# Modulation columns in two halves of the features, two of the k projections in two groups of matmuls, and a new order of the whole program

## The chip, the cores and the metric

The kernel runs on one core of a Trainium2 chip. The metric is the device time in microseconds (us) of one execution; three executions of the kernel before took 556.19 to 556.42 us, median 556.39. PE is TensorE, with PEld its loads of weights; DVE is VectorE, ACT is ScalarE, POOL is GpSimd, SP is SyncE, which here only issues DMAs.

## What is computed

An adaptive layer norm block on x of 2048 x 512: modulation vectors from a condition `c`, then linear attention with a learned softmax feature map of 32 heads, then a spatial-shift mixer with an MLP. Cut to its core:

```python
mod = (_silu(c) @ w_mod).reshape(1, 6, 1, 512)
sa, ca, ga, sb, cb, gb = (mod[:, i] for i in range(6))
h = _layernorm(x) * (1 + ca) + sa
q, k, v = h @ wqkv                           # per head: 16 columns each
pq, pk = q @ w_phi, k @ w_phi                # per head, 16 x 16
phi_q = concat([softmax(pq), softmax(-pq)])  # phi_k from pk in the same way
o = phi_q (phi_k^T v) / (phi_q phi_k^T 1)
x = x + ga * (o @ wo)
h = _layernorm(x) * (1 + cb) + sb
g = shift(gelu(_layernorm(h) @ w1)) @ w2     # quarters of the features shifted by +1, -1, +2, -2 rows
x1 = h + g
x = x + gb * (x1 + gelu(_layernorm(x1) @ w3) @ w4)
```

## The kernel before, in words

**Numbers.** Large products run in a fast float32 format. Each operand is split into a high part, a rounded copy, and a low part, the rest (`hi_lo`, L483: a copy and a subtraction), and each product is three matmuls (`three`, L474). Small products and transposes take plain float32; each of those matmuls shows in the trace as two records.

**An order that is written out.** The program is first recorded as a list of operations (`Plan`, `plan.op`, L314), each with its engine, what it reads and what it writes. Then it is emitted in the order of the printed table `ORDER` (L40), in which each number is an operation's index in that list and a letter behind it puts the operation on another of the engines that may do it (A for ACT, V for DVE, G for POOL). A second table, `SLOT`, names the buffer that each tile gets. Each engine works off its own operations in this order. So the order on each engine, the order of the DMAs on SP and the reuse of buffers are all set by the two tables; nothing is decided at run time but the waits. Tiles that share a kind of buffer (`KIND`, L34) can wait for each other: the kind `s2` holds raw weights, modulation rows, inputs and normed inputs alike, and `ps` is the eight PSUM banks (`pp`, `pt`, `pa`, `ac`).

**DMAs.** Loads go through `load` (L447) to SP's queue. Eight semaphores are used in turn, so a DMA is issued only after the eighth one before it has landed, besides waiting for its buffer.

**The start, up to the first projection.**
- `warm` (L500): nine groups of four matmuls on a tile of ones. Their results aren't used. What follows on TensorE stands behind them in the order.
- `load_folded` (L648), for wk and then wq: the feature map's 16 x 16 matrices are multiplied into the weights. For each of four blocks of 128 rows: a load of 256 KB (`rk`), four matmuls of 128 x 128 with a block-diagonal tile (`bd`) into a bank `pp`, and `hi_lo` into the weight tiles `w`.
- `layernorm` of the first four tiles of x (`xl` to `xn`).
- `mod_cols` (L529): the columns sa and 1 + ca that scale the first norm. silu(c) is spread to 32 columns (`wide`). Four loads of 512 KB bring 128 rows each of the first 1024 columns of w_mod (`mod2`); for each, four matmuls of 32 x 256 run beside each other in four strips of 32 rows of one bank. The bank is copied to SBUF (`r`), two transposes turn it into columns, and two `ts` write `cols`.
- `h_chunk` (L685) for chunk 0: transposes of `xn` into `pt` (two banks in turn, each for two of the four blocks of features), scale by 1 + ca and bias by sa, `hi_lo` into `hh`.

**The rest.** `proj` (L712) is 12 matmuls of 128 x 512 (four blocks of features, three each). Per chunk of two tiles `k_feat`, `v_feat` and `q_feat` project and take their softmaxes, and `kv_add` accumulates phi_k^T v in PSUM. Beside them run the rows of modulation (`mod_acc`, `mod_rows`), further loads and preparations of weights. Then come the attention's output, `pp<-w,oT` (wo), the second norm, `pa<-nT,w` (w1), `pp<-w,sh` (w2), and the MLP: `pa<-bH,wq` (w3) and `ac<-w,gg` (w4).

Of the kernel before, what the change touches and what calls it, by code (L numbers as in the profile page):

```python
# [11 lines left out]
OP = mybir.AluOpType  # L12
# [3 lines left out]
P = 128  # L16
NK = D // P
# [5 lines left out]
TPC = CH // P  # L23
# [141 lines left out]
)  # L165
SLOT = {
    "pp": "354206170301136260517505607442523070157475601660106031401453313745662015634523405103645651314210"
          "4326265450622670302462",
    "bd": "c3",
    "w": "124657de12834c6d075e18",  # L170
    "rk": "9768efjh",
# [1216 lines left out]
```

## Time and profile before

| | value |
|---|---|
| device time, median of 3 (lowest, highest) | 556.39 us (556.19, 556.42) |
| profiled execution: device time, span | 556.38 us, 554.6 us |
| instructions | 12399 |
| bytes moved, mean rate | 124.90 MB, 225 GB/s |
| granted TensorE clock, mean | 0.999 |

The span runs from the first to the last instruction of the engines; about 1.8 us of the device time lie around it. In the rows of the profile a name such as `pp<-w,hh` reads "into `pp` from `w` and `hh`", and `128*128 128x512` is a matmul of a 128 x 128 weight tile on 512 columns. Matmuls are pipelined, so that the mean duration of one is longer than the distance between two.

### The profile page before, as it was taken

What the parts mean: (1) busy time and instruction counts of PE and PEld (TensorE: products, weight loads), DVE (VectorE), ACT (ScalarE), POOL (GpSimd) and SP (SyncE); (2) the same over time, 40 slices, a digit from 0 to 9 for tenths busy, and PEclk for the clock granted to TensorE, in tenths of its full rate; (3) what the DMA queues carried; (4) which work ended last, traced back from release to release, by engine and by line L of the source; (5) the groups of instructions that cost most, each with busy time, mean ns of one, the idle gap of its engine ahead of it and who ended that gap; (6) DMA issues with size and microseconds to landing.
All of it is one profiled execution on the core that took longest, in us unless ns stands there. A gap on an engine that the chain in (4) does not pass through costs nothing.

```text
span 554.6 us, 12399 instructions
## 1 busy us (share of the span) xinstructions
PE 548.3 (99%) x4522; PEld 491.5 (89%) x4522; DVE 484.6 (87%) x901; ACT 352.1 (63%) x833; POOL 339.5 (61%) x348
## 2 busy tenths in 40 slices
PE   9999999999999999999999999999999999999997
PEld 8888788888777788888889999999999999999996
DVE  3899997999999999999898788788788777888876
ACT  4789988644344788978888786867352535235540
POOL 3289849788799999986986533516334453133522
PEclk9999999999999999999999999999999999999999
DMA  8964651654765668687898888896976796572212
GB/s 317 386 215 148 212 161 42 214 173 143 247 193 158 221 212 232 238 294 256 269 298 267 274 297 276 281 324 250 382 232 241 264 379 204 174 249 93 59 58 76
DMA packets 63749, 124.90 MB, mean 225 GB/s; under 512 B 7140, under 2 KB 26852, under 8 KB 59592
## 3 DMA queue, kind: packets, MB, share of 16 engines
q1 hardware_dynamic: 63400, 124.04, 67.3%
q8 instruction: 35, 0.57, 0.4%
q14 instruction: 26, 0.21, 0.1%
q10 hardware_dynamic: 288, 0.07, 0.1%
HBM read 89.74 MB, written 34.35 MB: 224 GB/s over the span
## 4 chain that ended last, share of the span: by engine, by line
PE 61%; DVE 1%; DVEq 0%; issue 0%
PE pa L471 26%; PE ac L471 20%; PE pp L471 14%; PE pt L480 1%; DVE pT L762 0%; DVE pp L437 0%; DVE xb L418 0%; DVEq L1384 0%; DVEq L418 0%; DVEq L762 0%
## 5 line engine op out<-in xcount | busy, mean ns | idle before, releaser
L471 PE MATMUL pp<-w,hh 128*128 128x512 f32 x576 | 137.9, 396 | 0.0
L471 PEld LDWEIGHTS pp<-w,hh 128*128 128x128 f32 x576 | 106.8, 188 | 25.6 <-ACT qe L401 0.8
L471 PE MATMUL pa<-bH,wq 128*128 128x256 f32 x840 | 107.7, 281 | 0.0
L471 PE MATMUL ac<-w,gg 128*128 128x256 f32 x840 | 107.2, 281 | 0.0
L471 PEld LDWEIGHTS ac<-w,gg 128*128 128x128 f32 x840 | 103.6, 188 | 1.2
L471 PEld LDWEIGHTS pa<-bH,wq 128*128 128x128 f32 x840 | 103.7, 189 | 1.0
L471 PE MATMUL pp<-w,sh 128*128 128x512 f32 x192 | 50.1, 399 | 0.0
L471 PE MATMUL pa<-nT,w 128*128 128x256 f32 x384 | 47.8, 282 | 0.9 <-DVE nT L418 0.6
L471 PEld LDWEIGHTS pa<-nT,w 128*128 128x128 f32 x384 | 46.5, 188 | 2.4 <-DVE nT L418 1.1
L471 PE MATMUL pp<-w,oT 128*128 128x512 f32 x192 | 47.7, 396 | 0.0
L471 PEld LDWEIGHTS pp<-w,oT 128*128 128x128 f32 x192 | 35.5, 188 | 8.1 <-DVE oT L418 0.4
L420 POOL TENSOR_TENSOR gg<-cu,gg 128x128 fp32r<-128x128 f32 (+1 forms) x29 | 19.0, 667 | 38.1 <-PE ac L471 18.4
L471 PEld LDWEIGHTS pp<-w,sh 128*128 128x128 f32 x192 | 34.5, 188 | 7.7 <-issue 1.0
L401 ACT ACTIVATE cu<-pa 128x512 f32<-128x512 f32 (+1 forms) x39 | 20.1, 519 | 27.5 <-PE pa L471 21.3
L588 POOL TENSOR_TENSOR rs<-mv,const 128x2 f32<-128x2 f32 x31 | 22.6, 732 | 24.3 <-ACT mv L595 23.0
L401 ACT ACTIVATE gg<-cu 128x256 fp32r<-128x256 f32 (+1 forms) x64 | 21.2, 357 | 23.7 <-PE ac L471 17.4
L420 POOL TENSOR_TENSOR e<-e,q 128x1024 f32<-128x1024 f32 x16 | 31.2, 1966 | 1.2 <-DVE q L418 1.1
L420 POOL TENSOR_TENSOR ez<-e,const 128x1024 f32<-128x1024 f32 x12 | 29.8, 2490 | 2.8 <-ACT const L401 2.8
L401 ACT ACTIVATE gg<-sg 128x512 fp32r<-128x512 f32 x37 | 22.5, 623 | 13.5 <-POOL sg L420 8.2
L418 DVE TENSOR_TENSOR gg<-sg,gg 128x512 fp32r<-128x512 f32 x38 | 26.8, 707 | 4.6 <-ACT gg L401 3.3
L401 ACT ACTIVATE cu<-cu 128x512 f32<-128x512 f32 (+1 forms) x36 | 19.3, 550 | 12.0 <-DVE cu L418 12.0
L418 DVE TENSOR_TENSOR cu<-pa,cu 128x512 f32<-128x512 f32 (+1 forms) x36 | 21.1, 593 | 6.4 <-PE pa L471 5.3
(214 smaller groups left out, 1212.4 us busy)
## 6 DMA issues: line engine op xcount, KB each, us to landing
wq<-dram SPq DMA_DIRECT2D x32, 1024.0 KB, 6.8
dram<-ws SPq DMA_DIRECT2D x35, 256.0 KB, 3.0
xl<-in_x SPq DMA_DIRECT2D x32, 256.0 KB, 4.3
dram<-qe SPq DMA_DIRECT2D x16, 512.0 KB, 2.9
e<-dram SPq DMA_DIRECT2D x64, 128.0 KB, 3.6
raw<-in_w SPq DMA_DIRECT2D x18, 256.0 KB, 3.9
mod<-in_wmod SPq DMA_DIRECT2D x16, 256.0 KB, 5.3
dram<-xl SPq DMA_DIRECT2D x16, 256.0 KB, 3.4
```

The lines of the kernel that those rows point to most:

```text
L401: nc.scalar.activation(o(), i(), func, **kw)
L418: dve = ("DVE", 71 + 1.04 * o.n + 90 * (isps(a) and isps(b)), lambda: nc.vector.tensor_tensor(o(), a(), b(), op=op))
L420: pool = ("Pool", cost, lambda: nc.gpsimd.tensor_tensor(o(), a(), b(), op=op))
L471: nc.tensor.matmul(o(), a(), b(), start=s, stop=e, **kw)
L480: nc.tensor.transpose(o(), i(), ident())
L588: plan.op("Pool", 540 + 10 * m, lambda: nc.gpsimd.tensor_tensor(r(), v(), mhalf[:, :m](), op=OP.pow), [r], [v, mhalf])
```

## The change

1. **`mod_cols`**: the features are done in two halves of 256. Each half has its own bank `p`, copy `r` and transposed bank `pc`; each of its four loads brings 128 rows of 256 columns of sa and 256 of 1 + ca (256 KB, in pieces of 1 KB, where before 512 KB came in pieces of 4 KB); the four matmuls of a load have 128 columns; one transpose and two `ts` of two columns finish each half. The loads of a half take the tag `mod`, so their buffers are of the kind `s2`.
2. **`k_feat`** takes `parts`, and chunk 0 calls it with 2: the projection's 12 matmuls are two operations of 6, one for each half of the features. The order can put other work between them.
3. **`ORDER` and `SLOT`** are printed anew for the whole program: 183 lines of them differ. The numbers in `ORDER` also shift because the operations are counted anew.

```diff
-    "0 3 45 12 38 2 240 10 46 7 47 48 87 13 49 242 239 30 26 53 57 55 39 59 34 40 1 41 4 22 241 42 43 6 50 243 "
...
-        p, r, pc = T("pp", [P, HD]), T("mod", [P, HD]), T("pp", [P, 2, P])
-        for k in range(NK):
-            raw = T("mod2", [P, 2, D])
-            load(raw, wmod_d[k * P:(k + 1) * P, :2 * D].rearrange("p (j n) -> p j n", j=2), 2 * P * D * 4)
-            mms([(p[32 * (2 * j + h):32 * (2 * j + h + 1)], wide[:, k, :], raw[:, j, h * HD:(h + 1) * HD], k == 0, k == NK - 1)
-                 for j in range(2) for h in range(2)], [p], [wide, raw], skip=True, tiles=4)
-        act(r, p, alts=("DVE",))
-        transp([(pc[:, i, :], r[:, i * P:(i + 1) * P]) for i in range(2)], [pc], [r])
-        for j in range(2):
-            ts(cols[:, j, :].re("p (h i) -> p h i", (2, 2), h=2).perm("p h i -> p i h", (1, 0)), pc[:, :, 64 * j:64 * (j + 1):32],
-               float(j), None, OP.add, None)
+        for h in range(2):
+            p, r, pc = T("pp", [P, P]), T("mod", [P, P]), T("pp", [P, P])
+            for k in range(NK):
+                raw = T("mod", [P, 2, HD])
+                load(raw, wmod_d[k * P:(k + 1) * P, :2 * D].rearrange("p (j h n) -> h p j n", j=2, h=2)[h], P * D * 4)
+                mms([(p[32 * (2 * j + q):32 * (2 * j + q + 1)], wide[:, k, :], raw[:, j, q * P:(q + 1) * P], k == 0, k == NK - 1)
+                     for j in range(2) for q in range(2)], [p], [wide, raw], skip=True, tiles=4)
+            act(r, p, alts=("DVE",))
+            transp([(pc, r)], [pc], [r])
+            for j in range(2):
+                ts(cols[:, j, 2 * h:2 * h + 2], pc[:, 64 * j:64 * (j + 1):32], float(j), None, OP.add, None)
...
-    def k_feat(hh, t, w, tt_):
+    def k_feat(hh, t, w, tt_, parts=1):
...
-        p = proj(rows(hh, t), w, mm, e)
+        p = proj(rows(hh, t), w, mm, e, parts=parts)
...
-        ks = [k_feat(hh, t, wk, c * TPC + t) for t in range(TPC)]
+        ks = [k_feat(hh, t, wk, c * TPC + t, 1 if c else 2) for t in range(TPC)]
```

**SP, the loads of the start.** Before, in the order of issue (`rk` are blocks of wqk, `mod` the loads of `mod_cols`, 1024 columns each):

```order
L448 DMA xl_106<-in_x 128x512
L448 DMA rk_108<-in_wqk_t 128x512
L448 DMA rk_110<-in_wqk_t 128x512
L448 DMA mod_20_112<-in_wmod 128x1024
L448 DMA mod_21_114<-in_wmod 128x1024
L448 DMA mod_22_116<-in_wmod 128x1024
L448 DMA mod_24_120<-in_wmod 128x1024
L448 DMA rk_122<-in_wqk_t 128x512
```

Now, from the eighth DMA of SP to the twenty-fifth, with what stands between left out as "...":

```order
L448 DMA rk_97<-in_wqk_t 128x512
L448 DMA rk_99<-in_wqk_t 128x512
L448 DMA rk_108<-in_wqk_t 128x512
L448 DMA rk_112<-in_wqk_t 128x512
L448 DMA rk_114<-in_wqk_t 128x512
L448 DMA mod_121<-in_wmod 128x2x256
...
L448 DMA mod_172<-in_wmod 128x2x256
L448 DMA mod_189<-in_wmod 128x512
L448 DMA rk_197<-in_wqk_t 128x512
L448 DMA rk_230<-in_wqk_t 128x512
L448 DMA mod_243<-in_wmod 128x2x256
...
L448 DMA mod_289<-in_wmod 128x2x256
```

All four blocks of wk (`rk_97`, `99`, `108`, `125`) and two of wq are now issued ahead of most of the modulation; the last load of the columns, which was SP's 11th DMA, is its 25th.

**PE, between the columns and the first k projection.** Before, one pass of columns (`pp_221`), its transposes into `pp_261`, then seven folds of which the first and the last stand here, then the k projection of tile 0 (`pp_354`):

```order
L471 MATMUL pp_221<-mod_24_120,const_210 32x256 x4
...
L480 MATMUL pp_261<-const_126,mod_252 128x128 x2
...
L471 MATMUL pp_272<-bd_162,rk_110 128x128 x4
...
L471 MATMUL pp_340<-bd_98,rk_166 128x128 x4
L471 MATMUL pp_354<-w_227,hh_291 128x512
```

Now, from the last fold (`pp_341`) on, with the transposes of `xn` cut to their first rows:

```order
L471 MATMUL pp_341<-bd_127,rk_230 128x128 x4
L480 MATMUL pt_351<-const_65,xn_143 128x128
...
L471 MATMUL pp_369<-mod_258,const_180 32x128 x4
L471 MATMUL pp_369<-mod_243,const_180 32x128 x4
L471 MATMUL pp_369<-mod_273,const_180 32x128 x4
L471 MATMUL pp_369<-mod_289,const_180 32x128 x4
L480 MATMUL pt_390<-const_65,xn_241 128x128
...
L480 MATMUL pp_401<-const_65,mod_395 128x128
L471 MATMUL pp_403<-w_210,hh_346 128x512
```

The first half of the columns (`pp_251`) stands far ahead of these rows, behind the fifth fold; the second half (`pp_369`) and its transpose (`pp_401`) stand behind the last fold and directly ahead of the first k projection (`pp_403`).

**ACT, the copy of the second half.** Now, ahead of the copy `mod_395<-pp_369` on ACT stand the eviction of a half of `hh`, two copies of folds and a scaling of a modulation row:

```order
L401 ACTIVATE hh_346<-pt_302 128x512
L401 ACTIVATE w_293<-pp_311 128x4x128
L401 ACTIVATE acc_366<-mod_189,const_134 128x512
L401 ACTIVATE w_293<-pp_341 128x4x128
L401 ACTIVATE mod_395<-pp_369 128x128
L401 ACTIVATE pt_359<-pt_359,const_307 128x256 x2
L401 ACTIVATE pt_390<-pt_390,const_307 128x256
```

Before, this copy was one instruction of DVE (`mod<-pp`, 128x256), with nothing queued ahead of it but the two evictions of the first fold.

**PE, where attention hands over to the wo projection.** Before, behind the wo projections of the first two tiles (`pp_2167`, `pp_2198`, 12 matmuls each) stand two q projections (`pp_2241`, `pp_2296`) with 16 small matmuls that spread a tile's `pT` ahead of each, then the wo projections of the next two tiles (`pp_2335`, `pp_2378`). In the middle of `pp_2378` stand the transposes of the second norm of the first two tiles (`pt_2393`, `pt_2398`). The first row of each group:

```order
L471 MATMUL pp_2198<-w_1173,oT_2118 128x512
...
L471 MATMUL pp_2241<-w_352,hh_1498 128x512
...
L471 MATMUL pp_2296<-w_352,hh_1217 128x512
...
L480 MATMUL pt_2393<-const_126,n_2268 128x128 x4
L480 MATMUL pt_2398<-const_126,n_2261 128x128 x4
```

Now one more q projection (`pp_2224`) stands behind the first two wo projections (`pp_2167`, `pp_2183`) and ahead of the transposes `pt_2429` and `pt_2435`:

```order
L471 MATMUL pp_2183<-w_1105,oT_2149 128x512
...
L471 MATMUL pp_2224<-w_293,hh_1410 128x512
...
L471 MATMUL pp_2285<-w_293,hh_1220 128x512
...
L471 MATMUL pp_2338<-w_293,hh_1410 128x512
...
L480 MATMUL pt_2429<-const_65,n_2255 128x128 x4
L480 MATMUL pt_2435<-const_65,n_2246 128x128 x4
```

Three q projections stand there now where two stood; the third was taken from between an earlier tile's `pT` matmuls and the first wo projection, where 12 matmuls are left of 24.

More of the change, by code (lines that the diff above doesn't have):

```diff
@@ L177 @@
-    "xn": "gbaba47ai968db2j",
-    "mod": "l6l76g452h91di45e2",
-    "mod2": "0213",
-    "kva": "2",
-    "za": "6",
-    "hh": "0839abc0",
-    "pt": "25327461613743570652324305736521",
-    "raw": "c21k18h7715djgf362a0fhae27gf",
-    "k1": "1045013501501501",
-    "ke": "5489712089712354",
-    "k2": "5234231243234323",
-    "vv": "a7dk85gac5hbb21h",
-    "qe": "6720487161942819",
-    "q1": "2330454052043312",
-    "qt": "kkbhb78bg11b",
-    "acc": "j3lcg",
-    "kvs": "2",
-    "pz": "7",
@@ new lines @@
+    "xn": "c07kgfd3g483djkj",
+    "mod": "ebeijd9hbilai40hkc856e60b1e",
+    "kva": "4",
+    "za": "5",
+    "hh": "3479bae3",
+    "pt": "00462115130761524043572301172014",
+    "raw": "413773fd3g5g7ki2hi8hcj14cfdg",
+    "k1": "1031420024315301",
+    "ke": "1036984763297410",
+    "k2": "0131312042042431",
+    "vv": "5bc210he0eali575",
+    "qe": "2254162959481134",
+    "q1": "2554550245102532",
+    "qt": "ggilik7hi6ig",
+    "acc": "2jfd1",
+    "kvs": "l",
+    "pz": "6",
+    "q2": "01231421",
@@ new lines @@
+    "e": "3867256958023578",
+    "ez": "7443377233952009",
+    "q3": "2345045025305340",
+    "q5": "34410342",
+    "pT": "8014329395105991",
+    "oT": "68ae8a26",
+    "nT": "b62b2962",
+    "n": "k66k0l2ilf722072",
+    "h": "37g491065efg3l86",
+    "gf": "74911911",
+    "sh": "93698c62",
+    "pa": "052345155071023162457107136013742513637025261470542130072516",
+    "wr": "70064",
+    "ws": "8g4l16a6jhbcbhieak0lle7a5klf60dh5aa",
+    "gb": "b",
+    "tw": "28285",
+    "bL": "07641782",
@@ new lines @@
+    "nb": "d7jdd7i502jh1i4k",
+    "yt": "ad30aidh15i99l8l",
+    "bH": "35493950120770576405619319374359",
+    "tr": "9ih05g65587f5le4",
+    "wq": "2e3c41937493174931974391743713479143",
+    "cu": "7eg20jhf5cd17l46igh5d3kfh097glc6e9i12d4k",
+    "gl": "de3i67kh",
+    "ac": "75244072615467423761064325013746",
+    "gg": "73890725398632981239026839450275368024173056437054590167841206738419256408361974",
+    "sg": "9f5933ca98a290fcc2c5425acd425lfg50hl4g65",
+    "xb": "iacke9ej183j8faj",
+    "xc": "7k3ed880aifggck0",
@@ L226 @@
+    "uu": "ghhgi74l",
 }
```

51 lines of the change are left out of this document (10 added, 41 removed), and 248 rows, old and new, of the table ORDER.

## The prediction, made before the changed kernel ran

> **What bounds the kernel now.** I read the page first, for the busy shares and the chain that ended last.
>
> ```profile
> PE 548.3 (99%) x4522; PEld 491.5 (89%) x4522; DVE 484.6 (87%) x901; ACT 352.1 (63%) x833; POOL 339.5 (61%) x348
> PE 61%; DVE 1%; DVEq 0%; issue 0%
> ```
>
> PE is busy 548.3 of 554.6 us, and the chain names hardly another engine. A share over the whole span hides stages, so next comes the table of windows by stage; its columns are busy us and instructions of PE, PEld, DVE, ACT and POOL, then granted clock, DMA share and GB/s.
>
> ```profile
> 0.00:11.90 11.90, 10.92 (x72) 10.93 (x73) 4.43 (x18) 6.02 (x16) 4.30 (x11) 1.00 0.86 303
> 11.90:23.20 11.30, 11.25 (x117) 9.99 (x115) 8.12 (x16) 6.03 (x16) 2.39 (x4) 1.00 1.05 389
> 60.00:160.00 100.00, 100.00 (x942) 80.64 (x939) 94.17 (x126) 63.01 (x134) 80.20 (x52) 1.00 0.56 175
> 160.00:215.00 55.00, 53.61 (x512) 42.90 (x512) 54.48 (x92) 38.13 (x86) 54.04 (x37) 1.00 0.61 187
> 350.00:550.74 200.74, 200.74 (x1650) 198.30 (x1649) 166.28 (x378) 95.27 (x231) 74.11 (x113) 1.00 0.64 219
> 550.74:554.60 3.86, 0.00 (x0) 0.00 (x0) 0.75 (x2) 0.00 (x0) 0.00 (x0) 0.79 0.36 121
> ```
>
> From 60 to 160 us and from 350 on, PE has no gap. It idles 0.98 us at the very start, 0.05 in the second window, 1.39 between 160 and 215, and 3.86 behind the last matmul. So the time is the moment PE begins its long run, plus PE's work, plus those gaps. DMAs, which the change edits most, count only where PE waits for them.
>
> **The start.** The timeline of PE (start, busy us, operation, records; a small matmul shows as two):
>
> ```profile
> 0.98 11.09 PE L471 MATMUL pp<-const 128*128 128x128 f32 x72 [0.98 <-POOL const L498]
> 11.90 1.06 PE L471 MATMUL pp<-bd,rk 128*128 128x128 f32 x8
> 13.56 1.93 PE L471 MATMUL pp<-mod,const 128*32 128x256 f32 x32
> 15.43 1.09 PE L480 MATMUL pt<-const,xn 128*128 128x128 f32 x8
> 16.36 0.38 PE L480 MATMUL pp<-const,mod 128*128 128x128 f32 x2
> 17.02 6.42 PE L471 MATMUL pp<-bd,rk 128*128 128x128 f32 x56
> 23.19 5.86 PE L471 MATMUL pp<-w,hh 128*128 128x512 f32 x24
> 28.88 1.04 PE L480 MATMUL pt<-const,xn 128*128 128x128 f32 x8
> 29.68 22.54 PE L471 MATMUL pp<-w,hh 128*128 128x512 f32 x96
> ```
>
> The first k projection starts at 23.19, behind nine warm groups, eight folds, the columns and four groups of transposes. All of it is still there after the change, so only two things can move the start: a wait inside this stretch, and work moved across the first projection. One group of four transposes is moved ahead of it (five now, four before): 0.80 us from 28.88 to 29.68 for two groups, so 0.40 for one. It is paid back later, so the mark to compare with is 23.19 + 0.40 = 23.6.
>
> **The change part by part.**
>
> *Column matmuls.* 32 records of 256 columns took 1.93 us, 0.060 each; now there are 64 of 128 columns. The nearest row on the other side has 64 columns in four strips:
>
> ```profile
> L471 PE MATMUL kva<-ke,vv 128*32 128x64 f32 x512 | 8.5, 220 | 0.0
> ```
>
> That is 0.0166 each. The ends are 64 x 0.0166 = 1.06 and 64 x 0.060 = 3.86, a change of -0.9 to +1.9. The line through both rows gives 0.031 for 128 columns, 1.98 in all. I take **+0.05**. The two transposes stay two.
>
> *Waits for loads.* How long a load takes to land, for the modulation's and for wk's and wq's in the first 24 us (min, median, max), with the issues' own durations and starts:
>
> ```profile
> DMA to landing us min/median/max: 5.3/5.4/7.5
> DMA to landing us min/median/max: 4.3/5.6/7.6
> L448 SPq DMA_DIRECT2D rk<-in_wqk_t x8: 327/426/432, 3.0 to 14.2; - x8
> ```
>
> The first fold now stands behind six warm groups. Before, nine ended at 11.9 and a group at full pace is 8 x 6.42/56 = 0.92 us, so six end near 9.15. The fold's load is SP's eighth; the first such load was the sixth, at 3.0, so it is issued near 3.9 and lands near 9.4 (8.2 to 11.5). A wait of 0.25 is what I take, estimated. Five folds and two warm groups (7 x 0.92) bring PE to the first columns at 15.8. Their last load is the 17th DMA, issued when the ninth has landed, 4.3 + 5.6 = 9.9, and there 5.4 later, at 15.3: no wait.
>
> The second half's last load is the 25th. Its semaphore comes free with the 17th, at 15.3, and its buffer with the first half's matmuls, near 16.5; 5.4 us later is **21.9**, at the longest 24.0. PE gets there after the first half (0.97), a warm group and three folds (3.7), the transpose (0.19) and four groups of transposes (1.7): 15.8 + 6.6 = **22.4**. Half a microsecond of slack, so no wait at the medians.
>
> *The second half on the way to k.* Its columns end at 23.4. Then come one group of transposes (0.4) and `pp_401`, which needs ACT's copy; k's first half follows. The rows of ACT and DVE for what stands there:
>
> ```profile
> 15.57 0.42 DVE L410 TENSOR_SCALAR mod<-pp 128x256 f32<-128x256 f32 x1 [1.16 <-PE pp L471]
> 11.72 0.29 ACT L401 ACTIVATE const<-const 128x128 f32<-128x128 f32 x1
> 17.22 0.99 ACT L401 ACTIVATE pt<-pt,const 128x256 f32<-128x256 f32 x2 [5.20 <-PE pt L480]
> 18.22 0.60 ACT L401 ACTIVATE hh<-pt 128x512 fp32r<-128x512 f32 x1
> 18.71 0.59 ACT L401 ACTIVATE w<-pp 128x512 fp32r<-128x512 f32 x1
> 25.31 0.71 ACT L401 ACTIVATE acc<-mod,const 128x512 f32<-128x512 f32 x1
> ```
>
> Ahead of the copy on ACT are hh, a fold's copy, the scaling and another copy: 0.60 + 0.59 + 0.71 + 0.59 = 2.5. The last of them waits for the last fold, near 21.5, so ACT is free by 22.1 to 23.3 and the copy (0.29) is done near 23.7. The group of transposes covers it: `pp_401` runs near 23.8 and k starts at **23.9**. Against 23.6 that is **+0.3**, of which 0.25 is the wait for the first fold. Below it the end is -0.05, the gap of before; above, a landing at 24.0 adds 1.6.
>
> This order also costs the edit its aim. If the second half stood behind k's first group, k could start some 1.4 us earlier in PE's order (the half's columns 1.0, the transposes 0.4), but PE would do the same work later; with PE dense on both sides nothing is gained. What the halves cover is only the eviction of hh's second half: two k groups of 6 x 0.235 (22.54/96) and one group of transposes are 3.2 us, from 23.9 to 27.1. Writing the columns (some 0.2, estimated), two scales that ACT does first (1.0), the half's own scale (0.5), hh (0.6) and its low part (0.7) end near 26.9. If that cover is short, k's second group waits some tenths.
>
> *Here a rule of the Trainium skill speaks against the change.* A load of these sizes beside its neighbours, by rate: from 8 to 9 us the 4 KB pieces of 512 KB loads, from 19 to 20 loads of 256 KB in 2 KB pieces, from 53 on the 1 KB pieces of `wr`:
>
> ```profile
> 8.00:9.00 1.00, 1.00 (x12) 1.00 (x11) 0.00 (x0) 1.00 (x3) 0.47 (x2) 1.00 1.04 397
> 19.00:20.00 1.00, 1.00 (x11) 1.00 (x10) 1.00 (x3) 0.97 (x3) 0.00 (x0) 1.00 1.05 387
> 53.00:54.00 1.00, 1.00 (x6) 0.83 (x6) 0.96 (x3) 1.00 (x3) 1.00 (x2) 1.00 0.99 330
> ```
>
> The Trainium skill ("DMA: Bandwidth & Descriptors", section "Measured (HBM→SBUF, 128 partitions, SWDGE, issued from GpSimd)") asks for DMAs of 1 MiB or more to reach three quarters of the peak; by it, 256 KB in place of 512 KB would slow the start. The trace doesn't bear that out for size: several loads lie in the queue at once, and 387 stands beside 397 GB/s. For the 1 KB pieces 330 against 387 makes eight loads, 2.1 MB, 0.9 us longer; half of it falls before the second half's last load needs it, and the slack of 0.5 takes it. I charge nothing and keep it for the rival.
>
> *From 23 to 160 us.* PE is dense, and DVE has some 6% to spare; instructions move between DVE, ACT and POOL. I find no wait that grows past its cover: 0.
>
> *Attention to wo, 160 to 215 us.* What PE's loads wait for there:
>
> ```profile
> PEld pp L471 <- DVE pT L762: 1.4, 4, 0.5
> PEld pa L471 <- DVE nT L418: 1.1, 2, 0.6
> PEld pt L480 <- ACT n L401: 1.0, 2, 0.8
> PEld pa L471 <- ACT nT L401: 0.7, 1, 0.7
> PEld pp L471 <- DVE oT L418: 0.4, 1, 0.4
> ```
>
> With "issue" 4.6 us are named, but only 1.39 reach PE. The second norm's transposes have another 12 matmuls, 2.8 us, ahead of them, which covers n: PE's share of that wait is
>
> ```profile
> 187.23 1.36 PE L480 MATMUL pt<-const,n 128*128 128x128 f32 x8 [0.33 <-ACT n L401]
> 190.98 2.98 PE L471 MATMUL pa<-nT,w 128*128 128x256 f32 x23 [0.34 <-DVE nT L418]
> ```
>
> 0.33. The nT waits keep their neighbours. Between pT and the first oT 2.8 us of matmuls are left of 5.6; how long the chain pT, attention, oT is, no row shows by itself, so its price lies between 0 and the 1.4 of the pT rows. DVE is busy 54.48 of 55, so whatever PE gains beyond 0.52 must be paid by less work on DVE. I take **-0.3**, with ends -1.4 and +1.4.
>
> *Behind 215 us.* PE is dense to the last matmul, the number of matmuls is the same, the tail's order too: 0.
>
> **Sum.** 556.38 + 0.05 + 0.3 - 0.3 = 556.4. The profiled execution (span 554.6, 1.8 around it) agrees with the median of 556.39, so no correction: **556.4**.
>
> **The rivals.**
> *Faster at the handover.* All of PE's 1.39 us of gaps go, since the order also moves copies from DVE to ACT (which is busy 38.13 of 55): 556.38 - 1.39 + 0.05 = 555.0. For it: DVE's rows head the waits, and the start might lose less than 0.3. Against: DVE at 54.48 and POOL at 54.04 are themselves nearly the bound. Chance 0.28.
> *Slower: the columns' second half comes late.* Issued behind the first half's matmuls near 16.5, it lands at 24.0 if it takes the longest time seen; PE needs it at 22.4. Price 1.6: 558.0. It decides from a landing past 22.4. For it: the 1 KB pieces (330 GB/s) and a queue that is full, 389 GB/s in the window. Against: medians of 5.4 and 5.6. Chance 0.14.
> *Slower: the first oT waits.* Half its cover is gone; at the 1.4 of pT's rows, 556.4 + 1.4 = 557.8. Against: the same 2.8 us stand ahead of the later oT, and that wait was 0.4 on PEld. Chance 0.10.
> *The change doesn't do what it says.* The halves start k no earlier, since both stand ahead of k in PE's order; then the time is that of before, 556.4. This is inside my forecast.
> *LDWEIGHTS as the measure.* In the window from 60 to 160 us PEld is busy 80.64 of 100, PE 100.00. If PE had slack there, the new order could win up to a fifth of it. But 96 matmuls of 512 columns in 22.54 us are 0.235 apart, and so they are wherever nothing waits: no slack. Chance 0.02, with a time some us lower. The Trainium skill ("Perfetto Trace Analysis", section "Identifying the Most-Contended Engine") holds matmul busy time to be a poor measure and takes LDWEIGHTS' instead.
>
> **How the numbers follow.** Forecast (no change that can be told) 0.46, from 555.3 to 557.5; faster 0.30 (0.28 + 0.02); slower 0.24 (0.14 + 0.10). What a measurement can tell here is about 0.2%, 1.1 us. The range for 8 in 10 takes in 555.0 and most of the slower cases: 554.8 to 557.9.
>
> **What would show it.** Right: the first projection's matmul between 23.6 and 24.2, PE's gaps up to there under 0.5, PE dense from 24 on, gaps of about 1 us between 160 and 215, and PE's long run ending within 1 us of 550.7. Wrong: a wait of PE for a `mod` load ahead of `pp_369`; a first fold that waits past 10 us; an oT wait over 1 us; a gap between 24 and 160 us, where I count on none.

## The result, and the profile after

| | before | after |
|---|---|---|
| device time, median (lowest to highest, runs) | 556.29 us (555.99 to 556.42, 4) | 559.88 us (558.58 to 560.75, 4) |
| profiled execution: device time, span | 556.38, 554.6 us | 560.75, 559.0 us |
| ratio after / before, 95% interval | | 1.0059, 1.0043 to 1.0075 |

The change makes the kernel 0.6% slower, some 3.6 us, where 556.4 and no measurable difference had been forecast. The profiled execution of after is the slowest of its four, so its shares are read against its own time.

The page of after, busy shares and chain:

```profile
PE 548.7 (98%) x4554; PEld 490.9 (88%) x4554; DVE 485.5 (87%) x885; ACT 355.9 (64%) x839; POOL 349.1 (62%) x361
PE 69%; DVE 13%; POOL 8%; DMA 5%; issue 3%; ACT 1%; SPq 0%; DVEq 0%; POOLq 0%; ACTq 0%
```

PE has hardly more to do (548.7 against 548.3 us), but the chain now runs through DVE for 13% and POOL for 8%, where it named DVE with 1% and POOL not at all. The windows by stage, with the columns of before's table:

```profile
11.90:24.11 12.21, 11.80 (x150) 10.80 (x149) 8.54 (x17) 10.20 (x25) 4.71 (x7) 1.00 0.99 339
60.00:160.00 100.00, 97.58 (x922) 78.25 (x920) 96.72 (x120) 60.33 (x129) 74.97 (x53) 1.00 0.47 147
160.00:215.00 55.00, 52.65 (x463) 41.90 (x453) 53.63 (x91) 37.68 (x88) 54.95 (x35) 1.00 0.74 230
350.00:555.28 205.28, 205.23 (x1692) 202.71 (x1690) 168.00 (x384) 99.03 (x238) 80.72 (x120) 1.00 0.63 219
```

Between 60 and 160 us, where PE had no gap, it now idles 2.42 us; DVE is busy 96.72 there, 94.17 before, with 120 instructions where 126 stood. Between 160 and 215 PE idles 2.35 (1.39 before). PE's timeline names the longer gaps:

```profile
23.20 0.43 PE L471 MATMUL pp<-mod,const 128*32 128x128 f32 x8 [0.41 <-DMA mod<-in_wmod]
...
24.11 1.65 PE L471 MATMUL pp<-w,hh 128*128 128x512 f32 x6
...
84.69 0.98 PE L480 MATMUL pt<-const,xn 128*128 128x128 f32 x7 [1.02 <-ACT xn L401]
85.96 14.17 PE L471 MATMUL pp<-w,hh 128*128 128x512 f32 x60 [0.29 <-ACT qt L401]
110.62 19.28 PE L471 MATMUL pp<-w,hh 128*128 128x512 f32 x82 [1.10 <-DVE hh L418]
167.21 1.16 PE L471 MATMUL pp<-pT,const 64*32 64x128 f32 x64 [0.49 <-DVE pT L762]
172.38 5.36 PE L471 MATMUL pp<-w,oT 128*128 128x512 f32 x22 [0.58 <-DVE oT L418]
192.84 1.09 PE L480 MATMUL pt<-const,n 128*128 128x128 f32 x8 [0.48 <-ACT n L401]
```

PE's last matmul ends at 555.28, 4.54 us later than before (550.74). PE's gaps up to there sum to 6.57 us in the timeline (2.42 before): that is 4.15 of it, and the column matmuls take 0.44 more. So the loss is gaps of PE, most of them waits for DVE and ACT. Of the 2.42 us between 60 and 160 us, 1.31 are for ACT's `xn` and `qt`, and 1.10 for DVE's `hh`.

### The profile page after: what moved, and what is told of

Read it like the earlier page. It is cut to its first block, busy times and chain, and to the rows that moved or that the text cites. A ratio compares the mean times of both kernels' runs of the same rounds, so it can differ in the third digit from the quotient of the medians.

```text
span 559.0 us, 12468 instructions
## 1 busy us (share of the span) xinstructions
PE 548.7 (98%) x4554; PEld 490.9 (88%) x4554; DVE 485.5 (87%) x885; ACT 355.9 (64%) x839; POOL 349.1 (62%) x361
## 4 chain that ended last, share of the span: by engine, by line
PE 69%; DVE 13%; POOL 8%; DMA 5%; issue 3%; ACT 1%; SPq 0%; DVEq 0%; POOLq 0%; ACTq 0%
PE pa L471 26%; PE pp L471 23%; PE ac L471 19%; DVE k L442 2%; DVE q L442 2%; POOL qe L420 2%; DMA dram<-h 2%; POOL ez L420 1%; PE pt L480 1%; POOL ke L420 1%; POOL e L420 1%; DMA wr<-in_w 1%; DMA mod<-in_wmod 1%; DMA e<-dram 1%; DVE za L418 1%
## 5 line engine op out<-in xcount | busy, mean ns | idle before, releaser
L471 PE MATMUL pa<-bH,wq 128*128 128x256 f32 x840 | 106.5, 281 | 0.0
L420 POOL TENSOR_TENSOR gg<-cu,gg 128x128 fp32r<-128x128 f32 (+1 forms) x22 | 14.4, 661 | 27.2 <-PE pa L471 13.3
L420 POOL TENSOR_TENSOR e<-e,q 128x1024 f32<-128x1024 f32 x15 | 29.9, 2013 | 0.6 <-DVE q L418 0.6
L401 ACT ACTIVATE qe<-qe 128x512 f32<-128x512 f32 x32 | 19.6, 626 | 16.4 <-POOL qe L420 12.7
L420 POOL TENSOR_TENSOR ke<-ke,k 128x1024 f32<-128x1024 f32 x13 | 27.0, 2083 | 2.8 <-DVE k L445 1.4
```

The source lines that it names most:

```text
L401: nc.scalar.activation(o(), i(), func, **kw)
L420: pool = ("Pool", cost, lambda: nc.gpsimd.tensor_tensor(o(), a(), b(), op=op))
L471: nc.tensor.matmul(o(), a(), b(), start=s, stop=e, **kw)
```

## The experiments

All edits are to the table `ORDER` of one of the two kernels, except for the halves alone; a number is an operation, a letter its engine. Each ratio is to the kernel before, run on the same chip in between.

### Taking PE's new waits away one by one

First theory: each gap has a misplaced instruction of its own, and moving it gives the gap's length back. Its rivals are the start (loads) and the amount of DVE's work. `a_same` is after unaltered. `a_xn` moves two copies of ACT that wait for a load to behind the `xn` that PE waits for. In after they stand ahead of it:

```profile
83.51 0.42 ACT L401 ACTIVATE ws<-wr 128x256 fp32r<-128x256 f32 x1 [2.30 <-DMA wr<-in_w]
83.83 0.80 ACT L401 ACTIVATE xn<-xl,nm,rs 128x512 f32<-128x512 f32 x1
```

`a_za` gives three of DVE's 1024-wide adds to POOL, and `a_start` issues wv's first load behind the last load of the columns.

```diff
a_xn
- 383 911 693 ... 418G 917 446 515 451
+ 383 693 ... 418G 446 515 911 917 451
a_za
- 230 298 ... 491 530 ... 670 686
+ 230G 298 ... 491G 530 ... 670G 686
a_start
- 44G 67 50 93 25 ... 61 71 178G
+ 44G 67 50 25 ... 61 71 93 178G
```

> The changed kernel unaltered (only the table's lines are wrapped anew), as the reference for the runs beside it and as a second profile. All theories: 558.6 to 560.8 us as in its four executions, median near 559.9. If the waits of PE at 83 to 86 us (transposes of xn, 1.0 + 0.3), at 109.5 (hh, 1.1) and at 167 to 172 (pT 0.5, oT 0.6) belong to the order, they are there again in this profile; if they were an accident of the one profiled execution, which was the slowest of four, some are gone.

> Changed kernel, but ACT does xn of chunk 6 and a hh copy ahead of the two ws operations that wait for the second wr load (it landed 6.5 us after its issue, and ACT stood 2.3 us). Theory ACT-blocked: PE's gaps of 1.0 + 0.3 at 83 to 86 us go and the time falls by 1.3, to about 558.6 if the reference is 559.9. Theory DVE-bound (DVE, slowed by POOL, is what PE waits for up to 215 us): the gap at 84 goes but comes back in front of hh at 110 or at the handover; the time moves by less than 0.4.

> Changed kernel, but three of the adds za<-za,ke (those of tiles 3, 8 and 14) go back from DVE to POOL, where the kernel before has them; 1.13 us each on DVE undisturbed, 2.4 on POOL. Theory DVE and POOL block each other (the add at 97.6 us took 1.75, the one at 100.1 took 2.31, ws behind it 2.16 in place of 0.33, each ending just behind a POOL operation): the wait for hh at 110 (1.1) goes, part of the handover's 1.1 too; the time falls by 1.1 to 2.0. Theory ACT-blocked or late start: less than 0.3 either way.

> Changed kernel, but the first load of wv (256 KB) is issued behind the columns' last load instead of three loads ahead of it. All theories: the wait of PE for the last modulation load (0.4 at 22.8 us) goes or halves. Theory late start carried to the end: the time falls by about 0.4. Theory DVE-bound or ACT-blocked later on: the gap is taken up by the waits at 84 to 110 us and the time moves by less than 0.2.

Measured: `a_same` 1.0080 (1.0058 to 1.0102), `a_xn` 1.0076 (1.0055 to 1.0097), `a_za` 1.0086 (1.0071 to 1.0102), `a_start` 1.0064 (1.0046 to 1.0081). The three edits lie within the interval of `a_same`. The `xn` wait went in `a_xn`, but also in `a_start` and `a_za`, whose order has the same two copies ahead of it: it comes and goes with the landing of one load. PE's wait for the columns' last load went in `a_start`, but in `a_xn` and `a_za` too, and the time doesn't show it. And less work on DVE gained nothing.

The second set takes on the other waits: `a_warm` puts two warm groups ahead of the first fold, `a_hh` moves a subtraction of DVE for `hh` ahead of others, `a_chain` moves two instructions on DVE's way to `pT`, and `a_all` has these three, `a_start` and `a_xn`.

```diff
a_warm
- 18 49 27 59 ... 52G 260 10 20G ... 261 4 102
+ 18 49 10 4 27 59 ... 52G 260 20G ... 261 102
a_hh
- 895G 581 457 ... 811 576 1163
+ 895G 581 576 457 ... 811 1163
a_chain
- 474 398 702 408 723 400 ... 668 813 816G ... 731 907
+ 474 702 408 723 398 400 ... 668 816G ... 731 813 907
```

> Changed kernel, but eight of the nine warm groups stand ahead of the first fold, as nine did before, so that TensorE doesn't reach the fold before its load has landed. So far the changed kernel was 3.6 and 4.8 us slower than the kernel before, and PE waited 0 to 1.4 us there. Theory late start carried to the end: the first k projection starts at 23.3 to 23.9 in place of 23.9 to 25.0, and the time falls by the same 0.4 to 0.7, to about 3.5 over the kernel before. Theory DVE's order (PE waits later on for single operations of DVE): the start is earlier, but the waits at 109 and 167 us grow by as much; the time stays at about 4 over.

> Changed kernel, but DVE's subtraction for the low part of hh_1220's first half (its high part was written at 91 us, the subtraction runs at 109.9, behind 16 other operations) stands directly behind that of the other half. Theory DVE's order: PE's wait of 1.1 at 109.5 goes and stays gone; the marks behind it (first matmul on kvs, last matmul) come 1.1 earlier against the start of k. Theory DVE-bound as a whole: the wait goes there, but the waits for pT and oT grow by 0.5 to 1.1, and the end stays where it was within 0.3.

> Changed kernel, but two moves on DVE ahead of the first attention tiles: the subtraction qe is put behind DVE's ez, so that ez (3.4 us, of which 2.2 behind POOL's ez, which starts 0.4 earlier and reads SBUF too) comes first, and one reduction of 1.2 goes behind the normaliser of the first two tiles. Theory blocking at the port, on the way to pT: ez takes 1.2, pT is ready 2 to 3 us earlier, the waits for pT (0.5) and oT (0.6) go; time 1.1 lower. Theory DVE-bound: pT's wait goes, but oT's stays or others take its place; less than 0.4.

> Changed kernel with all five moves: warm groups ahead, wv's first load behind the columns' loads, xn ahead of ws on ACT, hh's subtraction earlier, ez and a reduction moved. If the slowdown is the sum of single waits made by the order (0.7 at the start, 0 to 1.3 at xn, 1.1 at hh, 1.1 at pT and oT), 3 to 4 of the 4 us go and the time is 556.5 to 557.5, within 1 of the kernel before. If DVE's sum of work sets the pace up to 215 us, at most 1 us goes: over 559.

Measured: `a_warm` 1.0057 (1.0034 to 1.0079), `a_hh` 1.0051 (1.0038 to 1.0064), `a_chain` 1.0085 (1.0058 to 1.0113), `a_all` 1.0083 (1.0054 to 1.0112). In `a_warm` the first k projection starts at 23.89 as meant, and the time stays that of after. In `a_hh` PE's wait for `hh` near 110 us is gone as meant, but its waits of that trace now read:

```profile
PE pp L471 <- POOL ke L420: 0.8, 1, 0.8
PE pp L471 <- DVE pT L762: 0.8, 1, 0.8
```

A new wait of 0.8 at 149 us and a longer one for `pT` took its place, and the matmuls of `pT` begin at 167.3 as in after (167.2). In `a_chain` the wait for `pT` is 1.2, longer than in after. In `a_all`, too, the wait for `hh` is gone, and there those for `ke` and `pT` are 1.2 and 1.4. With all five moves the sum of the gaps was to go, and the time is that of `a_same`. The theory of independent gaps falls: something behind the gaps is late.

### What is late: DVE, standing behind POOL

DVE's short addition `const<-pp,const`, ahead of PE's matmuls on `pT`, serves as a mark (in before both of DVE's transposes of `pT` stand ahead of it, in after one). A window from the first k projection to that mark, of before (PE, PEld, DVE, ACT, POOL):

```profile
23.19:161.29 138.10, 138.10 (x1118) 111.00 (x1117) 131.53 (x181) 97.37 (x218) 113.58 (x82) 1.00 0.57 180
```

The same window of after:

```profile
24.11:165.18 141.07, 138.66 (x1113) 110.44 (x1113) 135.36 (x179) 95.59 (x210) 107.94 (x79) 1.00 0.53 173
```

The stretch is 3.0 us longer, DVE has two instructions less and is "busy" 3.8 us longer. So its instructions last longer. Which ones do shows only when DVE's and POOL's timelines are laid over each other. Before:

```profile
98.57 0.41 DVE L418 TENSOR_TENSOR ws<-wr,ws 128x256 fp32r<-128x256 f32 x1
...
99.44 1.21 DVE L418 TENSOR_TENSOR za<-za,ke 128x1024 f32<-128x1024 f32 x1
...
101.47 1.07 POOL L420 TENSOR_TENSOR ws<-ws 128x256 fp32r<-128x256 f32 x1 [3.91 <-DVE ws L418]
...
102.46 1.20 DVE L442 TENSOR_REDUCE k<-ke 128x64 f32<-128x1024 f32 x1
102.50 1.94 POOL L420 TENSOR_TENSOR ke<-ke,k 128x1024 f32<-128x1024 f32 x1
103.58 0.68 DVE L418 TENSOR_TENSOR hh<-pt,hh 128x512 fp32r<-128x512 f32 x1
```

After, at the same place and at 151 us:

```profile
99.89 1.48 POOL L420 TENSOR_TENSOR w<-raw,w 128x512 fp32r<-128x512 f32 x1
...
100.14 2.31 DVE L418 TENSOR_TENSOR za<-za,ke 128x1024 f32<-128x1024 f32 x1
...
101.33 2.92 POOL L420 TENSOR_TENSOR ke<-ke,k 128x1024 f32<-128x1024 f32 x1
...
102.37 2.16 DVE L418 TENSOR_TENSOR ws<-wr 128x256 f32<-128x256 f32 x1
...
104.45 0.68 DVE L418 TENSOR_TENSOR hh<-pt,hh 128x512 fp32r<-128x512 f32 x1
...
151.23 2.74 POOL L420 TENSOR_TENSOR ez<-e,const 128x1024 f32<-128x1024 f32 x1 [1.55 <-issue]
151.62 3.43 DVE L418 TENSOR_TENSOR ez<-e,const 128x1024 f32<-128x1024 f32 x1
```

Before, DVE's adds on SBUF fall at this place where POOL idles (3.91 us, while it waits for a `ws`), and beside POOL's `ke` DVE runs a reduction of one operand and a subtraction from PSUM (`pt`): all at their undisturbed durations. After, an addition or subtraction of DVE that starts while POOL's instruction runs ends about its own length behind POOL's end: POOL's `w` ends at 101.37 and DVE's `za` at 102.45, 1.1 later (1.21 us by itself); POOL's `ke`, started at 101.33 while that `za` runs, lasts 2.92 instead of 1.94 and ends at 104.25, 1.8 behind `za`; DVE's `ws`, 0.41 by itself, ends at 104.53, 0.28 behind `ke`; DVE's `ez` ends at 155.05, 1.1 behind POOL's at 153.97. These three of DVE exceed their undisturbed lengths by 1.1, 1.75 and 2.2 us, and a `za` at 97.58 (1.75 us) does by 0.5: 5.6 us in all. In before the whole stretch has 1.4, in three instructions of about 1.2 us by themselves:

```profile
96.78 1.87 DVE L418 TENSOR_TENSOR za<-za,ke 128x1024 f32<-128x1024 f32 x1
120.28 1.61 DVE L418 TENSOR_TENSOR ke<-ke,k 128x1024 f32<-128x1024 f32 x1
129.17 1.56 DVE L418 TENSOR_TENSOR za<-za,ke 128x1024 f32<-128x1024 f32 x1
```

Without what it stood, DVE's busy time in the two windows is the same, 130.1 and 129.8 us.

The Trainium skill ("SBUF — State Buffer", section "SBUF: two separate sides") states the rule: DVE and GpSimd share a pair of ports, and an instruction of GpSimd, or one of DVE that has two inputs in SBUF (against one of GpSimd that reads SBUF) or runs in a two-port mode, takes the pair whole for all its length; the later one is blocked. The trace agrees in the pairs shown here: the later one's time grows by nearly what was left of the earlier one (DVE's `ez` by 2.2 us, with POOL's ending 2.35 us behind its start). In `a_za` a DVE instruction with one operand in SBUF (`ws<-ws`, a TENSOR_SCALAR of 0.29 us) was held to 2.49 us by POOL's `za`.

This also explains `a_za`: three adds less on DVE, but three more on POOL for it to meet. From the first k projection to the mark DVE is busy 136.1 us there, with 176 instructions, against 135.4 with 179 in after. And in `a_chain`, where `ez` went ahead and kept its 1.23 us, the next instruction behind it stood in its place:

```profile
149.92 1.23 DVE L418 TENSOR_TENSOR ez<-e,const 128x1024 f32<-128x1024 f32 x1 [0.53 <-ACT const L401]
151.06 3.42 DVE L418 TENSOR_TENSOR qe<-qt,q 128x1024 f32<-128x1024 f32 x1
```

### Taking the collisions out of after

Port theory: the instructions that collide, moved to the engine on which they don't, give the time back, whatever the number of instructions on DVE. `a_port1` gives three of DVE's additions and subtractions at 99.7 to 104.5 us (two of them the collisions above) to POOL; `a_port2` brings POOL's `ez` of 151 us to DVE, which has **more** to do then; `a_port12` does both; `a_best` adds `a_warm`, `a_start`, `a_xn` and `a_hh`.

```diff
a_port1
- 580 912 410 913 ... 456 898 315
+ 580 912G 410G 913 ... 456 898G 315
a_port2
- 723 400 725G 724
+ 723 400 725 724
```

> Changed kernel, but three operations of DVE at 97 to 104 us that read two operands from SBUF and there end just behind a POOL operation (za<-za,ke_903, ws_1134, ws_1326: 1.13 + 0.4 + 0.4 us of work, 2.85 more of standing behind POOL) go to POOL. Theory DVE sets the pace to the attention and POOL's operations hold it up: DVE's busy time between the first k projection and the mark const<-pp,const falls from 135.4 to about 131 us, the mark comes 2.5 to 4 us earlier against the start, the time falls to 1 to 2 us over the kernel before. Theory collisions only move on (as with the three adds moved to POOL, where DVE's own work fell by 3.3 us and its busy time did not): busy stays over 134, the time over 3 us above.

> Changed kernel, but POOL's first ez (ez_1927) goes to DVE behind DVE's own ez, which stood 2.2 us behind it. Theory DVE's pace and POOL's hold-up: DVE's busy time falls by 1.0 (2.2 less of standing, 1.2 more of work), POOL's by 2.4; the time falls by 1.0. Theory collisions move on: within 0.5 of the changed kernel.

> Changed kernel with both of these. DVE's pace and POOL's hold-up: DVE's busy time near 130.5 as in the kernel before (130.6), the mark const<-pp,const at 161 to 162.5, the time 556.5 to 558. Collisions move on: over 559.

> Changed kernel with both of these, and the warm groups ahead, wv's first load later, xn ahead of ws and hh's subtraction earlier. DVE's pace and POOL's hold-up: now PE's own waits count, since DVE is no longer late: 0.5 to 1 below a_port12, 556 to 557.5. If a_port12 has not gained, neither does this.

Measured: `a_port1` 1.0044 (1.0026 to 1.0062), `a_port2` 1.0049 (1.0032 to 1.0066), `a_port12` **1.0021** (1.0007 to 1.0035, median 557.46), `a_best` 1.0026 (1.0015 to 1.0037). Neither half alone can be told from after by its time; both together can. In `a_port2` DVE does both `ez` one after the other, each at 1.2 us:

```profile
149.96 2.35 DVE L418 TENSOR_TENSOR ez<-e,const 128x1024 f32<-128x1024 f32 x2
```

Two on one engine take 2.35 us; one on each took DVE alone 3.43. The windows from k to the mark for `a_port1`, `a_port2` and `a_port12`:

```profile
24.36:164.36 140.00, 138.57 (x1113) 110.57 (x1113) 131.06 (x176) 95.61 (x210) 109.47 (x82) 1.00 0.53 176
24.22:162.31 138.09, 137.09 (x1108) 109.41 (x1108) 134.06 (x179) 95.77 (x210) 104.64 (x77) 1.00 0.54 178
23.80:161.75 137.95, 137.37 (x1108) 109.64 (x1108) 130.00 (x177) 95.65 (x210) 106.80 (x81) 1.00 0.54 179
```

With both it is 137.95 us long, as in before (138.10), and the mark stands at 161.75 (after 165.18). PE's wait for `hh` is gone, and that for `pT` too, without either being touched. By ratio (1.0059 to 1.0021) some 2.1 of the 3.6 us come back. `a_best` adds nothing that can be measured, where 0.5 to 1 us less had been expected.

The halves differ in what they free. `a_port2` takes out the one collision of 2.2 us at 151 us: its window is already as short as before's, PE's waits for `pT` and `oT` are gone, and the wait for `hh` (1.00 us at 109) stays. `a_port1` takes out 2.85 us at 100 to 104 us: the wait for `hh` goes, but the mark comes only 1.1 us earlier against the start of k, where 2.5 to 4 had been expected, and those for `pT` (0.69) and `oT` (0.61) stay. DVE was busy 131.06 us, as expected, but it now stood idle for 2.47 us at 112 us, waiting for a `ke` of ACT. By these two traces the late mark of after comes mostly from the last collision, and PE's wait for `hh` from the earlier ones.

### The halves alone, and a shorter warm-up, in the kernel before

`b_halves` is before with the columns in two halves (eight loads of 256 KB in pieces of 1 KB, matmuls of 128 columns), the second half's operations directly behind the first's, at the place of the one pass. Both halves share the one bank, the one buffer for its copy and the 512 KB buffers of before, so the new kind of buffer and `k_feat` in two groups aren't in it. `b_warm6` is before without three of the nine warm groups, so that the first fold stands behind six as in after (twelve matmuls whose result isn't used are left out).

```diff
b_warm6
- 246 9 247 95 44G 11 14 249 15 8 251
+ 246 247 95 44G 14 249 15 251
```

> The kernel before with one thing of the change alone: the modulation's columns in two halves of the features (eight loads of 256 KB, eight groups of matmuls with 128 columns, two copies, two transposes, four short ts), both halves one after the other at the place of the one pass of before; the order is that of before. It tells what part of the slowdown the halves have by themselves. Theory (up to the attention DVE sets the pace, and the change lost its time where DVE's operations stand behind POOL's): the halves lengthen the start by 0.3 to 0.6 us (column matmuls 2.37 us in the trace of after, 1.93 before), no operation of DVE meets another of POOL than before, so the mark of DVE's const<-pp,const before pT comes 0.3 to 0.8 later than in before and the time is before + 0.2 to 0.8 us (ratio 1.000 to 1.002). Rival (the halves themselves are the cost, by their loads or their columns): before + 2 us or more.

> The kernel before without the last three of its nine warm groups (twelve matmuls whose result isn't used are left out), so that the first fold stands behind six groups, as in the changed kernel. It tells whether an earlier start is worth anything when the order behind it is that of before. If PE sets the pace: first fold near 9.2 to 9.6 (its load decides), the columns wait for their loads for up to 1.5 us, first k projection 1 to 2.5 us earlier than 23.2, and the time is before - 0.5 to -2 us. If DVE sets the pace up to the attention (its work between the first k projection and the mark const<-pp,const is as long as PE's, less some idle time): k earlier, but the mark before pT moves less than half as much, PE gets gaps behind 60 us, and the time is before - 0.5 to +0.5 us.

Measured: `b_halves` 0.9997 (0.9988 to 1.0006): the halves themselves, with their eight loads in pieces of 1 KB, cost nothing that can be measured, less than the 0.2 to 0.8 us that the port theory had expected. `b_warm6` is **slower**, 1.0022 (1.0012 to 1.0033): both of its theories said otherwise. PE's timeline of its start:

```profile
0.97 7.60 PE L471 MATMUL pp<-const 128*128 128x128 f32 x48 [0.97 <-POOL const L498]
10.08 1.13 PE L471 MATMUL pp<-bd,rk 128*128 128x128 f32 x8 [1.51 <-issue]
12.05 1.09 PE L480 MATMUL pt<-const,xn 128*128 128x128 f32 x4 [0.84 <-DMA const<-in_id]
13.06 3.05 PE L471 MATMUL pp<-mod,const 128*32 128x256 f32 x32
...
23.80 5.83 PE L471 MATMUL pp<-w,hh 128*128 128x512 f32 x24
```

Two windows of its start, and the second of them in before:

```profile
12.00:13.00 1.00, 0.95 (x4) 0.72 (x4) 0.66 (x1) 0.00 (x0) 0.97 (x2) 0.50 1.00 391
13.00:16.00 3.00, 3.00 (x33) 1.31 (x32) 0.00 (x0) 0.00 (x0) 0.00 (x0) 0.60 1.05 389
13.00:16.00 3.00, 2.99 (x41) 1.91 (x42) 1.80 (x3) 0.00 (x0) 0.16 (x1) 1.00 1.08 397
```

Waits of 1.51 and 0.84 us open where the warm groups were, and behind them the granted clock is 0.50 from 12 to 13 us and 0.60 from 13 to 16, where it is 1.00 in before: the same 32 records of columns last 3.05 us instead of 1.93. The first k projection starts at 23.80, 0.6 later than in before, and from there on every mark of PE is 0.5 later up to `pT`. So in this trace of before's order PE sets the pace, and the later start is passed on.

### Collisions put into the kernel before

The positive control: DVE's instructions of before in another order on DVE; the order of every other engine stays. `b_coll` moves a `za` add and a `w<-raw,w` by some 3 us, to where POOL's `ke` ran. `b_coll2` moves a `ws<-ws` of 0.4 us back behind one instruction, into POOL's `za`, and a `w<-raw,w` of 145.7 us ahead to 141, into POOL's next `za`. `b_coll3` has all four.

```diff
b_coll
- 395 396 899 ... 791 402 561 ... 625 454 629
+ 395 899 ... 791 561 ... 625 454 396 402 629
b_coll2
- 671 784 544G 785 635 574 ... 1143 649 382 ... 687 660 386
+ 671 544G 635 784 785 574 ... 1143 649 660 382 ... 687 386
```

> The kernel before with a collision put in: on DVE one add za<-za,ke and one subtraction ws<-w,raw, which in before run while POOL stands idle (97.6 to 101.5 us), are moved behind DVE's reciprocal of a later k, where POOL's ke<-ke,k runs (102.5 to 104.4). Same work, same engines. Port theory (a DVE operation with two operands in SBUF and a POOL operation exclude each other for a whole instruction): one of the two moved operations, or POOL's ke, lasts 1 to 2 us longer than undisturbed, DVE's mark const<-pp,const comes 0.5 to 2 us later, and as before has some 2 us of slack there the time is before + 0.3 to 1.5 us. Rival (only the order of work on PE and ACT counts): the durations stay as they were, and the time is within 0.3 us of before.

> The kernel before with larger collisions put in, nearer to the attention: DVE's ws<-ws (0.42 us at 123.1) is moved one instruction back, behind DVE's first k<-pp of the tile that follows, so that it meets POOL's za<-za,ke (123.4 to 125.8); and the first of DVE's two w<-raw,w of 145.7 is moved behind DVE's reciprocal of 140.9, where POOL's next za<-za,ke runs (139.9 to 142.3). Same work, same engines; an add of 0.3 us is moved by half a microsecond. Port theory: the ws<-ws lasts 2.0 to 2.5 us, the w<-raw,w 1.4 to 2.2 us, everything of DVE behind the first is 1.5 to 2.1 us later than in before until idle time takes it up (DVE has 2 us of it from 100 to 161), the mark const<-pp,const before pT comes 0.5 to 3 us later, and the time is before + 0.3 to 2 us. Rival (durations do not depend on the other engine): both durations as in before, mark and time within 0.3 us of before.

> b_coll and b_coll2 in one kernel: four operations of DVE moved in the kernel before, some 4 us of hold-up by the port theory, as much as the changed kernel has. Port theory: mark const<-pp,const 1.5 to 4 us later than in before, PE gaps of 1 us and more ahead of pT, time before + 1 to 3 us. Rival: within 0.3 us of before. If the mark comes late and the time does not, the idle time of the other engines hides what the port costs here, and the collisions alone are not enough for the slowdown.

Measured: `b_coll` 1.0007 (0.9996 to 1.0018), `b_coll2` **1.0052** (1.0037 to 1.0068; 559.51 us), `b_coll3` 1.0070 (1.0054 to 1.0085; 560.07). The place in `b_coll2`, DVE and POOL:

```profile
123.37 0.69 DVE L442 TENSOR_REDUCE k<-pp 128x32 f32<-128x512 f32 x1
123.58 2.39 POOL L420 TENSOR_TENSOR za<-za,ke 128x1024 f32<-128x1024 f32 x1 [2.56 <-DVE za L418]
123.97 2.28 DVE L418 TENSOR_TENSOR ws<-ws 128x256 fp32r<-128x256 f32 x1
125.93 0.93 POOL L420 TENSOR_TENSOR ws<-ws 128x256 fp32r<-128x256 f32 x1
126.18 1.21 DVE L442 TENSOR_REDUCE k<-ke 128x64 f32<-128x1024 f32 x1
```

In before the same `ws<-ws` stands ahead of that reduction and of POOL's `za`, and takes 0.42 us:

```profile
123.13 0.42 DVE L418 TENSOR_TENSOR ws<-ws 128x256 fp32r<-128x256 f32 x1
123.36 2.46 POOL L420 TENSOR_TENSOR za<-za,ke 128x1024 f32<-128x1024 f32 x1 [2.55 <-DVE za L418]
```

Half a microsecond in the order costs DVE 1.9 us. The moved `w<-raw,w` lasts 1.49 instead of 0.68, and the late DVE makes a collision nobody put there (a `za` at 131 us, 2.36 instead of 1.56). The mark comes at 164.87, 3.6 us late, and PE's longest waits up to `pT` are 1.25 us, for POOL, and 0.61, for the mark itself. The window from k to the mark is that of after nearly to the number:

```profile
23.26:164.87 141.61, 139.92 (x1123) 111.96 (x1121) 134.50 (x180) 97.08 (x217) 115.06 (x83) 1.00 0.54 177
```

Both durations came as the port theory had said; the mark and the time came later than it had said (0.5 to 3 and 0.3 to 2 us), and so they did in `b_coll3`: its mark stands at 165.74, and it is 4.0 us slower, where 1 to 3 had been expected. One of PE's gaps in that trace is a wait of 1.52 us at the start, ahead of any of the moves.

`b_coll` tells the rest: its two instructions lost 0.9 us together (1.54 and 1.22 us instead of 1.21 and 0.68), and the mark stands at 161.16, as in before (161.29). The port theory had expected 1 to 2 us on one of them, a mark 0.5 to 2 us late and at least 0.3 us of time. The hold-up came, but smaller, and it was taken up: at 122 us 0.2 us of it is left, since 0.22 us of DVE's idle time is gone and its collision at 120 us is shorter (a `ke` of 1.36 instead of 1.61). So a hold-up costs what idle time and shorter collisions behind it don't take: `b_coll2`'s mark is 3.6 us late, and 3.4 us show in the time.

## Why the prediction was wrong, point by point

- **Column matmuls, +0.05**: mis-sized. 64 records of 128 columns took 2.37 us (1.08 + 0.86 + 0.43), 1.93 before: +0.44. The line through 64 and 256 columns gave 0.031 each; 0.037 was measured. It lies inside the ends, and `b_halves` shows no cost of it in the time.
- **First fold's wait, 0.25**: not in the profiled execution, whose fold started at 8.95 without a wait; its load had been put at 9.4. In the variants with the same order there it started between 9.2 and 9.8, behind waits of 0 to 1.4 us.
- **Second half's last load, no wait**: wrong by 0.41. PE reached it at 22.8, not 22.4, and it came at 23.2, not 21.9. It was issued at 17.45, where 16.5 had been worked out, so the issue was late by 1 us; its way of some 5.7 us lay near the medians of 5.4 and 5.6. The rival that priced this at 1.6 us came with a quarter of it.
- **First k projection at 23.9**: it started at 24.11, and between 23.8 and 25.0 in the variants. The time was right by some luck: the wait in it was 0.41 for the `mod` load and not 0.25 for the fold. And the second group of k followed without a wait, so the halves did cover the second half of `hh`.
- **LDWEIGHTS as the measure, and size or pieces of loads**: neither decides. PE's k projections keep their distance, and `b_halves` has the small loads and loses nothing.
- **"From 23 to 160 us: 0"** is the step that failed. The reasoning was that PE is dense, that DVE has 6% to spare, and that no wait grows past its cover. The work is nearly the same; what it runs beside is not. Of DVE's collisions with POOL the forecast said nothing, although before's own trace has them (a `za` of 1.21 us that lasted 1.56 at 129 us), and none of its rivals names them. DVE stood some 4 us longer behind POOL than before (5.6 against 1.4), its mark came 3.9 us late (0.9 of them from the start), and PE idled 2.4 us between 60 and 160 where it had not idled at all: 1.1 for `hh`, which goes with the collisions (`a_port1`, `a_port12`), and 1.3 for ACT behind a load, which comes and goes between the variants.
- **Attention to wo, -0.3**: wrong sign. Gaps of PE between 160 and 215 us went from 1.39 to 2.35. The wait for the first `oT`, a rival, came with 0.58 instead of 1.4, a wait for `pT` of 0.49 joined it, and n's wait, which 2.8 us of further matmuls should have covered, went from 0.33 to 0.48. The `pT` wait is a consequence of the late mark (it is gone in `a_port2` and `a_port12`, and `oT`'s with it but for 0.2 us in the latter); n's remains there. The 4.6 us that the forecast names for PE's loads are the five rows shown, without "issue"; nothing hangs on it. Its argument that DVE at 54.48 of 55 us has nothing to spare took busy time for work.
- **Behind 215 us, 0**: nearly. Gaps of 0.4 us near 304, and between 0 and 1.5 us in the variants.

The 1.3 us that `a_port12` still loses stay open. Its trace, of an execution 0.8 us slower than its median, has gaps of PE that before has not: 0.6 us more at the start, 0.6 for ACT's `xn` and `qt`, 0.5 and 0.4 behind 215 us. No run had after's order with before's start, so none tells which of them the median holds.

None of these versions is faster than the kernel before.

## What to carry to other kernels

When a change writes a new order, lay the engines that share a port over each other in the trace before you call a stretch unchanged: for every VectorE instruction with two operands in SBUF, and for one that copies or rounds from SBUF to SBUF, ask which GpSimd instruction runs at that moment, and place it beside GpSimd's idle time, or give GpSimd its turn while VectorE reads PSUM. A busy share counts the time in which an instruction stands blocked, so compare durations of the same instruction, not shares. And when several waits appear at once and each edit only moves them, look for the late engine behind them. Look last at what follows a hold-up: 2.85 us taken out where DVE had idle time behind it moved the mark by 1.1 us, 2.2 us taken out close to the wait by 3.0.

## What the runs showed of the hardware that was not expected

- An exchange of two neighbouring instructions (`b_coll2`) makes one of 0.42 us last 2.28 us, and together with one more move on the same engine it makes the kernel 0.5% slower.
- POOL is blocked in the same way: its `ke<-ke,k` lasts 1.94 us alone and 2.92 behind DVE's `za`.
- The granted clock was 0.50 from 12 to 13 us and 0.60 from 13 to 16, behind two waits of 1.51 and 0.84 us with one fold between them (`b_warm6`; its mean clock was 0.994 to 0.997 in all eight executions, against 0.998 to 1.000 for the kernel before beside it); a single wait of 1.52 us at the same place in `b_coll3` left the columns at 1.93 us, their full pace. The Trainium skill ("TensorE: Matmul & The Clock Gate", section "HAM oscillation — how this bites in real kernels") warns of idle gaps over about 3.4 us; in this trace shorter ones, close together, were enough.
